# A work order searched anew with other VectorE and buffer costs, and q's weights loaded in three parts

## The chip, the core and the metric

The kernel runs on one core of a Trainium2 chip. TensorE (PE) multiplies, VectorE (DVE) and ScalarE (ACT) empty PSUM and do the elementwise work, GpSimd (POOL) applies masks, and SyncE (SP) issues nearly all DMAs. The metric is the device time of one execution in microseconds; a profile of one execution gives every instruction's start and duration on its own span.

## The reference

Two attention blocks on two inputs of 2048 tokens by 640 features, with 32 heads of 20 features; the outputs stand side by side, 1280 columns wide.

```python
# A: sliding window of 256 tokens
q, k, v = split(A_x @ A_wqkv)
p = softmax(where(0 <= i - j < 256, q @ k.T * 20 ** -0.5, -1e9))
a = (p @ v) @ A_wo
# B: linear attention
q, k, v = split(B_x @ B_wqkv)
phi = lambda t: where(t > 0, t + 1, exp(t)) + 1e-6
kv, z = phi(k).T @ v, phi(k).sum(tokens)
b = ((phi(q) @ kv) / (phi(q) @ z + 1e-6)) @ B_wo
out = concatenate([a, b], -1)
```

## The kernel before

The tokens go in four tiles of 512 (four blocks of 128). All operands are bfloat16, sums are float32 in PSUM.

**A.** Per tile, `proj_pad` (L496) makes q and k with the features in the partitions, five groups of five 512-column products each (L511). The first four groups hold even heads; what belongs to the odd heads goes to DRAM and back in a `relay` (L541, L534, L544, on SP). `proj_v` (L555) makes v (L566). A score *unit* (`unit`, L600) is one head group with part of a tile's key blocks: up to 64 small products in row tiles (L620), two exponentials on ScalarE (L641 for three of four heads, L644 for the fourth), and masks on GpSimd, or on VectorE where the plan says so (L665, L668, L669, L663). There are 96 units; every three give a *value group* (`values`, L689; products in column tiles, L698), copied out (L711) and stored to `orelay` (L730). When a tile's eight value groups are stored, `a_norm` (L740) reads them back (L753, L754), divides, and `finish_rows` (L786, products L796) multiplies by `wo`, copies (L804, L802) and stores to the output (L810).

**B.** `b_keys` (L861, L873) makes 32 key groups of 320 columns, `phi` (L817) follows each. `phi` has two ways: ScalarE takes the exponential straight from PSUM (L826), or VectorE first copies the sum out (L832) and ScalarE works on the copy (L843); then VectorE takes the minimum (L846) and the maximum (L849). `b_sums` (L909) sums over all tokens, `b_kvwo` (L981, L998) folds `wo` in and passes the result through DRAM to `kvwo`, and `b_query` (L1049, L1057, then L796) makes the queries and the result.

**Order of the work.** Nothing of the order is decided on the chip. While the program is built, a planner (`Planner`, L81) keeps a time for every engine and DMA, takes for each engine the ready operation with the lowest key, and emits it; the engines then run these orders strictly, waiting on semaphores. The table `K` (L20) holds the keys, the pace of the units, and the earliest times of DMAs. An operation's planned duration is a formula (`dve_sb`, L256; `phi.min` and `phi.max` at L834 and L835). PSUM offers three fill banks (with the scores' banks when they are free), handed out in turn; a group of products needs the bank whose last user has been read out. Four output buffers (`osb`), four `e` buffers and three `ost` buffers go in rings (`take`, `give`; L235, L236), whose slot the planner counts free at the giving operation's end, for a DMA its landing plus a pad.

**The start.** Ten warm-up products (L1087) run ahead in a fill bank. SP loads x of tile 0 in four blocks (`load_x0`, L455), which TensorE transposes (L470) and VectorE or ScalarE copies (L479). The weights of q and k each come in two column parts, 160 and 480 columns (`load_turned`, L1102), and are copied into their final column order, one copy per group (L1120, L1118). All other tiles of x are transposed by the DMA, five loads per tile (`load_x`, L435; issue at L442). A tile of x takes one of four slots in turn and waits for its former user. B's key weights `wk` are loaded from SP (L1132, L1141).

Of the kernel before, what the change touches and what calls it, by code (L numbers as in the profile page):

```python
# [7 lines left out]
P = 128  # L8
# [5 lines left out]


K = {
    "units": (10.0, 2.45, 0.814, 0.583, 1.081),
    "slack": (0.39, 1.89, 0),
    "defer": 1.27,
    "q0": (-80.4, 1.09),  # L20
    "k0": (-76.5, 0.43),
    "x": (-4.4, -5.1, -9.3, 6.8, 36, 57.2, 100),
    "xb": (129.4, 27.91),
    "w": (1.6, 23.7, 103.0),
    "rows": (86.9, 44, 84, 86.4),
    "pad": 1.41,
    "v0": (-22.4, 0.4),
    "v1": (-69.9, 1.3),
    "q1": (17.3, 1.62),
    "k1": (27.1, 0.69),  # L30
    "b0": (9.7, 0.62),
    "b1": (25.7, 1.09),
    "b2": (55.6, 0.65),
    "b3": (83.3, 0.35),
    "g": (71.6, 7.42),
    "q2": (96.5, 4.88),
    "k2": (45.3, 6.49),
    "v2": (84.0, 1.3),
    "z": (109.3, 0.64),
    "kvwo": (143.1, 1.98),  # L40
    "q3": (116.9, 1.76),
    "k3": (140.6, 0.89),
    "v3": (145.2, 2.04),
    "bq0": (158.1, 2.9, 197.3, 1.46),
    "bq1": (210.9, 4.71, 196.4, 4.76),
    "bq2": (195.1, 0.28, 244.4, 4.78),
    "bq3": (190.6, 2.38, 257.0, 1.47),
    "ao": (8.5, 1.61),
}


# [29 lines left out]
class Planner:  # L81
# [101 lines left out]
    def run(self):  # L183
        while True:
            best = None
            for e, ops in self.avail.items():
                if not ops:
                    continue
                f = self.free.get(e, 0.0)
                t0 = INF  # L190
                for o in ops:
                    s = self._start_time(o, f, e)
                    if s < t0:
                        t0 = s
                if t0 == INF:
                    continue
                t = max(f, t0)
                pick = None
                for o in ops:
                    if self._start_time(o, f, e) <= t + 1e-9:  # L200
                        k = (self._rank(o, t), o.ready)
                        if pick is None or k < pick[0]:
                            pick = (k, o)
                if best is None or t < best[0]:
                    best = (t, e, pick[1])
            if best is None:
                break
            t, e, o = best
            for x in o.engs:
                self.avail[x].remove(o)  # L210
            dur = o.engs[e]
            if e == "PE" and o.mode != self.mode:
                dur += self.SWITCH
                self.mode = o.mode
            if o.group is not None and o.first:
                p = self._bank(t)[1]
                o.group["bank"] = (p, p["next"])
                o.group["pool"] = p["pool"]
                o.group["tag"] = p["tag"]
                p["ends"][p["next"]] = INF  # L220
                p["next"] = (p["next"] + 1) % len(p["ends"])
            for r, h in o.take:
                h["i"] = r["next"]
                r["ends"][r["next"]] = INF
                r["next"] = (r["next"] + 1) % len(r["ends"])
            self.free[e] = t + dur
            o.emit(e)
            if o.mb is not None:
                self.data = max(self.data, t + dur) + o.mb
                self.sent += [self.data + self.LAND] * o.n  # L230
                o.end = self.data + self.LAND + o.pad
            else:
                o.end = t + dur + (self.LAT[e] if o.lat is None else o.lat)
            self.log.append((t, dur, e, o))
            for r, h in o.give:  # L235
                r["ends"][h["i"]] = o.end  # L236
            if o.group is not None and o.last:
                p, i = o.group["bank"]
                p["ends"][i] = o.end
            for s in o.succ:  # L240
                s.ready = max(s.ready, o.end)
                s.left -= 1
                if s.left == 0:
                    self._push(s)
        assert not any(self.avail.values())
# [19 lines left out]
def kernel(  # L265
# [108 lines left out]
            self.users.append(ops)  # L374


    def group(mms, evac, key, deps=(), shape=None, dtype=F32, chunk=2, name="", mode="full"):

        g = {}
        name = name or mms[0][1].__qualname__.split(".<locals>.")[1]  # L380
        prev = None
        n = len(mms)
        i = 0
        first = True
        while i < n:
            part = mms[i : i + chunk]

            def emit(e, part=part, first=first):
                if first:
# [4 lines left out]
            o = pl.op({"PE": sum(m[0] for m in part)}, emit, key if first else -1000, list(deps) if first else [prev], lat=0.0 if i + chunk < n else None, group=g, name=name)  # L394
# [101 lines left out]
    def proj_pad(t, i, key0, dkey):  # L496
# [11 lines left out]
        for c in range(KT):  # L508
            def mk(kt, c=c):
                def m(ps):  # L510
                    nc.tensor.matmul(ps[:], lhsT=wA[i][:, kt, c * P : (c + 1) * P], rhs=xb["t"][:, kt, :], start=(kt == 0), stop=(kt == KT - 1))  # L511
# [305 lines left out]
    def phi(g, n, dst):  # L817
# [5 lines left out]
        def e1(e):  # L823
# [6 lines left out]
            else:  # L830
                st["t"] = epool.tile([P, n], BF16, name="t")
                nc.vector.tensor_copy(out=st["t"][:], in_=g["ps"][:])  # L832
                x = pl.op({"ACT": act_t(n)}, e2, PHK, [o1], name="phi.exp")
            o3 = pl.op({"DVE": 0.14 + 0.00026 * n}, e3, EVK if e == "ACT" else PHK, [x], name="phi.min")  # L834
            o4 = pl.op({"DVE": dve_ps(n) if e == "ACT" else 0.17 + 0.00104 * n}, e4, EVK if e == "ACT" else PHK, [o3], name="phi.max")  # L835
            if e == "ACT":
                o4.group = g
                o4.last = True
# [263 lines left out]
    def load_turned(i, eng, key):  # L1102
# [1 line left out]
        raw = over.tile([P, KT, D], BF16, name="raw", tag=f"K{2 + i}")  # L1104
        v = a[:, :, i * D : (i + 1) * D]
        ld = [load_w(eng, raw[:, :, 0:160], v[:, :, 0:160], key, 0.9, pad=0.5)]
        ld.append(load_w("SP", raw[:, :, 160:], v[:, :, 160:], key + 1, 2.3, pad=0.5))
        wA_op[i] = []
        for c in range(KT):
            def em(e, c=c):  # L1110
# [8 lines left out]
                else:  # L1119
                    nc.vector.tensor_copy(out=d, in_=s)  # L1120

            wA_op[i].append(pl.op({"DVE": dve_sb(D), "ACT": act_t(D)}, em, -5000 if i == c == 0 else -3900 + 2 * c + i, ld[0:1] if c == 0 else ld, name="wturn"))

    load_turned(0, "ACTQ", -99.5)
    load_turned(1, "SP", -99)
# [93 lines left out]
```

## Time and profile before

| | |
|---|---|
| median of 11 runs | 274.89 us (270.7 to 276.0) |
| profiled execution | 275.45 us, its span 273.7 us |
| granted TensorE clock, mean | 0.981 |
| busy: PE, DVE, ACT, POOL | 257.0 (94%), 197.0 (72%), 215.0 (79%), 138.1 (50%) us |
| instructions: PE, DVE, ACT, POOL | 4086, 385, 283, 251 |
| masks on POOL, L668 and L669 | 91 each, mean 673 and 726 ns |
| `phi.min` L846, 320 columns | x32, mean 403 ns |
| `phi.max` L849 from the copy, 320 columns | x22, mean 573 ns |

The span runs from the first to the last instruction; the 1.75 us between it and the execution's time lie around it. A line of the profile names line, engine, operation and tiles; "SPq" is SP's queue issuing a DMA; a bracket at the end holds the engine's idle time ahead of the instruction and what ended it.

### The profile page before, as it was taken

Reading aid. Unit: us, or ns where it says so; the run is one execution under the profiler, and the core shown is the slowest. Engines: PE = TensorE matmul, PEld = TensorE weight load, DVE = VectorE, ACT = ScalarE, POOL = GpSimd, SP = SyncE. Lnnn points to the kernel's source line nnn. Section 1 sums busy time; section 2 is a strip of 40 time slices with the busy share of each in tenths; the row PEclk is TensorE's granted clock in tenths of the full one; section 3 lists DMA queues with packets and bytes.
Section 4 is the critical chain, followed back from the end, with each engine's and each line's share of the span. In section 5 each row is a group of like instructions: output and inputs, shape, how many; then the busy total and the mean of one; then the engine's idle time right before and its main releaser. Section 6 shows DMA issues by size and latency. Waiting matters only on the chain.

```text
span 273.7 us, 9682 instructions
## 1 busy us (share of the span) xinstructions
PE 257.0 (94%) x4086; PEld 153.3 (56%) x4114; DVE 197.0 (72%) x385; ACT 215.0 (79%) x283; POOL 138.1 (50%) x251
## 2 busy tenths in 40 slices
PE   8899999999849999999999999999998899999995
PEld 4336764555514556666555666656555556556673
DVE  2746699978845897634485673667889998789654
ACT  2583099899964998888889888888989899999540
POOL 5056046666553375655555655577783565640000
PEclk9999999999965999999999999999999999999999
DMA  7976969578562494960033367965595234512532
GB/s 206 292 115 118 220 129 215 88 113 235 127 124 57 96 336 131 192 107 22 23 96 100 74 151 210 179 124 109 130 209 181 72 85 103 151 46 69 162 134 96
DMA packets 55996, 37.13 MB, mean 136 GB/s; under 512 B 33681, under 2 KB 55185, under 8 KB 55953
## 3 DMA queue, kind: packets, MB, share of 16 engines
q1 hardware_dynamic: 55297, 36.32, 56.9%
q8 instruction: 32, 0.52, 0.8%
q10 hardware_dynamic: 656, 0.20, 0.3%
q14 instruction: 11, 0.09, 0.1%
HBM read 16.42 MB, written 12.88 MB: 107 GB/s over the span
## 4 chain that ended last, share of the span: by engine, by line
PE 75%; DVE 13%; DMA 6%; issue 2%; SPq 1%; ACT 1%; DVEq 0%; ACTq 0%
PE F L511 16%; PE F L796 13%; PE s L620 9%; PE F L909 8%; PE F L566 8%; PE F L698 8%; PE F L873 5%; PE F L1049 4%; DVE pq L849 3%; DMA raw<-in_A_wqkv_dram 2%; DVE e L846 2%; DVE t L832 2%; DMA xT<-in_A_x_dram 2%; DVE osb L804 2%; DVE ost L711 1%
## 5 line engine op out<-in xcount | busy, mean ns | idle before, releaser
L641 ACT ACTIVATE p<-s 128x1536 bf16<-128x1536 f32 (+2 forms) x96 | 131.8, 1373 | 25.1 <-PE s L620 19.8
L668 POOL TENSOR_SCALAR_AFFINE_SELECT p<-p 128x512 bf16<-128x512 bf16 x91 | 61.3, 673 | 76.4 <-ACT p L641 75.9
L669 POOL TENSOR_SCALAR_AFFINE_SELECT p<-p 128x512 bf16<-128x512 bf16 x91 | 66.1, 726 | 0.0
L511 PE MATMUL F<-xT,wA 128*128 128x512 bf16 x184 | 50.4, 399 | 5.5 <-DMA xT<-in_A_x_dram 2.0
L644 ACT ACTIVATE p<-s 128x512 bf16<-128x512 f32 (+2 forms) x96 | 54.8, 573 | 0.0
L620 PEld LDWEIGHTS <-kpad 20*128 20x128 bf16 x1440 | 21.2, 93 | 31.8 <-issue 30.0
L620 PE MATMUL s<-qpad,kpad 20*128 20x128 bf16 x1440 | 37.6, 219 | 1.3 <-ACT p L641 0.7
L511 PEld LDWEIGHTS <-wA 128*128 128x128 bf16 x200 | 18.1, 100 | 25.4 <-issue 7.9
L711 DVE CAST ost<-F 128x512 bf16<-128x512 f32 x30 | 20.7, 690 | 14.2 <-PE F L698 12.8
L804 DVE CAST osb<-F 128x320 bf16<-128x320 f32 x49 | 23.3, 486 | 8.1 <-PE F L796 6.3
L873 PE MATMUL F<-wkq,xT 128*128 128x320 bf16 x160 | 25.9, 300 | 1.2 <-DVE ost L711 0.8
L1049 PE MATMUL F<-xT,wq 128*128 128x512 bf16 x91 | 24.2, 382 | 2.3 <-DVE t L832 1.0
L698 PE MATMUL F<-p,v 128*32 128x128 bf16 x1440 | 26.0, 220 | 0.1
L796 PE MATMUL F<-woA,oT 128*128 128x320 bf16 x160 | 24.1, 299 | 1.3 <-DVE t L832 1.0
L566 PE MATMUL F<-wA,xT 128*128 128x320 bf16 x160 | 24.8, 299 | 0.0
L665 POOL TENSOR_SCALAR_AFFINE_SELECT p<-p 128x512 bf16<-128x512 bf16 x16 | 10.9, 705 | 26.7 <-ACT p L641 26.7
L796 PE MATMUL F<-kvwo,pq 128*128 128x320 bf16 x160 | 23.5, 299 | 0.2 <-DVE pq L849 0.2
L698 PEld LDWEIGHTS <-v 128*32 128x32 bf16 x1440 | 20.5, 97 | 5.0 <-issue 2.5
L846 DVE TENSOR_SCALAR e<-e 128x320 bf16<-128x320 bf16 (+1 forms) x52 | 20.6, 402 | 2.8 <-ACT e L843 1.6
L832 DVE CAST t<-F 128x320 bf16<-128x320 f32 (+1 forms) x34 | 18.7, 553 | 3.5 <-PE F L1049 1.9
L525 DVE CAST kpad<-F 128x512 bf16<-128x512 f32 x16 | 11.1, 691 | 13.5 <-PE F L511 13.3
L796 PEld LDWEIGHTS <-oT 128*128 128x128 bf16 x160 | 15.1, 98 | 7.9 <-issue 1.2
(77 smaller groups left out, 302.2 us busy)
## 6 DMA issues: line engine op xcount, KB each, us to landing
out_dram<-osb SPq DMA_DIRECT2D x32, 160.0 KB
orelay<-ost SPq DMA_DIRECT2D x32, 128.0 KB
oT<-orelay SPq DMA_DIRECT2D x8, 320.0 KB
qpad<-relay SPq DMA_DIRECT2D x16, 80.0 KB
kpad<-relay SPq DMA_DIRECT2D x16, 80.0 KB
xtok<-in_B_x_dram SPq DMA_DIRECT2D x2, 640.0 KB
xT<-in_B_x_dram SPq DMA_DIRECT2D x2, 640.0 KB
raw<-in_A_wqkv_dram SPq DMA_DIRECT2D x2, 600.0 KB
```

Of the source, the lines that this page charges most:

```text
L511: nc.tensor.matmul(ps[:], lhsT=wA[i][:, kt, c * P : (c + 1) * P], rhs=xb["t"][:, kt, :], start=(kt == 0), stop=(kt == KT - 1))
L566: nc.tensor.matmul(ps[:], lhsT=xb["t"][:, kt, b * P : (b + 1) * P], rhs=wA[2][:, kt, hf * HALF : (hf + 1) * HALF], start=(kt == 0), stop=( ...
L620: nc.tensor.matmul(o, lhsT=kt_[HD * j : HD * j + Dh, hg, ko : ko + P], rhs=qbox["t"][HD * j : HD * j + Dh, hg, b * P : (b + 1) * P], start ...
L641: nc.scalar.activation(out=st["p"][:, 0:3, :, :], in_=st["s3"][:, :, 0 : nb * P].rearrange("p h (k q) -> p h k q", q=P), func=ACT.Exp, sca ...
L644: nc.scalar.activation(out=st["p"][:, 3, :, :], in_=st["s1"][:, 0 : nb * P].rearrange("p (k q) -> p k q", q=P), func=ACT.Exp, scale=scale)
L668: nc.gpsimd.affine_select(out=p[:, :, 0, :], in_=p[:, :, 0, :], pattern=[[0, 4], [-1, P]], compare_op=ALU.is_ge, fill=0.0, base=-1, channe ...
L669: nc.gpsimd.affine_select(out=p[:, :, 1, :], in_=p[:, :, 1, :], pattern=[[0, 4], [1, P]], compare_op=ALU.is_ge, fill=0.0, base=0, channel_ ...
L698: nc.tensor.matmul(ps[HD * j : HD * j + HD, b * P : (b + 1) * P], lhsT=vA[kb]["t"][:, h * HV : h * HV + HD], rhs=pst["p"][:, j, x, :], sta ...
L796: nc.tensor.matmul(ps[:], lhsT=lhs(c), rhs=rhs(c, hf), start=(c == 0), stop=(c == KT - 1))
L804: nc.vector.tensor_copy(out=d, in_=ps[:])
L873: nc.tensor.matmul(ps[:], lhsT=xb["t"][:, kt, b * P : (b + 1) * P], rhs=R["wk"][:, kt, hf * HALF : (hf + 1) * HALF], start=(kt == 0), stop ...
L1049: nc.tensor.matmul(ps[:], lhsT=R["wq"][:, kt, :].rearrange("p (f c) -> p c f", c=KT)[:, c, :], rhs=xb["t"][:, kt, :], start=(kt == 0), sto ...
```

## The change

- **Planner.** `phi.min` and `phi.max` are planned longer (0.14 to 0.25 us and 0.17 to 0.21 us of fixed cost). A ring slot given back by a DMA counts free at the landing, without the pad that other readers wait.
- **Table.** All keys and earliest times are new, `defer` is doubled. Every engine's order changes from the first instructions on. `phi` takes ScalarE's way in 26 of 52 cases instead of 18; of the value copies all 32 stand on VectorE instead of 30.
- **Weights of q.** Three parts: 160 columns on ACT's queue as before, 160 and then 320 columns on SP. Each of the first two groups' copies waits for its own part only.
- **First group of q.** Twenty products of 128 columns, block by block, each block waiting for its own transposed block of x, instead of five of 512 columns.
- **Warm-up.** Five products up front and two placed by the planner between the transposes, in a bank of the scores, instead of ten.
- **`wk`.** Issued from ACT's queue with a very low key, so at its earliest time.

```diff
@@ K (cut)
-    "units": (10.0, 2.45, 0.814, 0.583, 1.081),
+    "units": (12.8, 2.45, 0.773, 0.56, 1.081),
-    "defer": 1.27,
+    "defer": 2.54,
-    "q0": (-80.4, 1.09),
-    "k0": (-76.5, 0.43),
-    "x": (-4.4, -5.1, -9.3, 6.8, 36, 57.2, 100),
-    "xb": (129.4, 27.91),
-    "w": (1.6, 23.7, 103.0),
+    "q0": (-69.9, 0.2),
+    "k0": (-60.2, 0.38),
+    "x": (-8.2, -3.7, -13.5, 1.6, 29.7, 57.2, 100.0),
+    "xb": (135.8, 22.84),
+    "w": (12.5, 36.7, 114.7),
...
@@ Planner.run
-                r["ends"][h["i"]] = o.end
+                r["ends"][h["i"]] = o.end - o.pad
@@ group(..., more=())
-            o = pl.op(..., list(deps) if first else [prev], ...)
+            o = pl.op(..., list(deps) if first else [prev, *more[i // chunk]] if more else [prev], ...)
@@ proj_pad
-            g = group([(mm_t(NQ), mk(kt)) for kt in range(KT)], [(either(NQ), ev)], key0 + c * dkey, deps=list(xb["ready"]) + [wA_op[i][c]] + (need if c < 4 else []))
+            if t == i == c == 0:
+                def mb(b, kt):
+                    def m(ps):
+                        q = slice(b * P, (b + 1) * P)
+                        nc.tensor.matmul(ps[:, q], lhsT=wA[0][:, kt, 0:P], rhs=xb["t"][:, kt, q], start=(kt == 0), stop=(kt == KT - 1))
+                    return m
+
+                g = group([(mm_t(P), mb(b, kt)) for b in range(TB) for kt in range(KT)], [(either(NQ), ev)], key0, deps=xb["ready"][0:1] + [wA_op[0][0]], chunk=KT, more=[[r] for r in xb["ready"]])
+            else:
+                g = group(...)
@@ phi
-            o3 = pl.op({"DVE": 0.14 + 0.00026 * n}, ...)
-            o4 = pl.op({"DVE": dve_ps(n) if e == "ACT" else 0.17 + 0.00104 * n}, ...)
+            o3 = pl.op({"DVE": 0.25 + 0.00026 * n}, ...)
+            o4 = pl.op({"DVE": dve_ps(n) if e == "ACT" else 0.21 + 0.00104 * n}, ...)
@@ start
-    nwarm = 10
+    wt = s3pool.tile([P, 3, NQ], F32, name="s3")
 
     def warmup(e):
-        w = fpool.tile([P, NQ], F32, name="F", tag="bank0")
-        for _ in range(nwarm):
-            nc.tensor.matmul(w[:], lhsT=warm[:, 0:P], rhs=warm[:], start=True, stop=True)
-
-    warmup("PE")
+        nc.tensor.matmul(wt[:, 0, :], lhsT=warm[:, 0:P], rhs=warm[:], start=True, stop=True)
+
+    for _ in range(5):
+        warmup("PE")
+    for at in (3.75, 4.4):
+        pl.op({"PE": 0.43}, warmup, 0, earliest=at)
...
-    pl.free["PE"] = 4.9
+    pl.free["PE"] = 3.4
@@ load_turned
         ld = [load_w(eng, raw[:, :, 0:160], v[:, :, 0:160], key, 0.9, pad=0.5)]
-        ld.append(load_w("SP", raw[:, :, 160:], v[:, :, 160:], key + 1, 2.3, pad=0.5))
+        if i == 0:
+            ld.append(load_w("SP", raw[:, :, 160:320], v[:, :, 160:320], -98.9, 0.9, pad=0.5))
+        r = 160 * len(ld)
+        ld.append(load_w("SP", raw[:, :, r:], v[:, :, r:], key + 1, 1.7 + i * 0.6, pad=0.5))
...
-            wA_op[i].append(pl.op(..., ld[0:1] if c == 0 else ld, name="wturn"))
+            wA_op[i].append(pl.op(..., ld[c : c + 1] if c < len(ld) - 1 else ld, name="wturn"))
@@ wk
-    wk_op = dma("SP", em_wk, 3.0, -94, at=K["w"][0])
+    wk_op = dma("ACT", em_wk, 3.0, -9000, at=K["w"][0])
```

More of the change, by code (lines that the diff above doesn't have):

```diff
@@ L16 @@
 K = {
-    "units": (10.0, 2.45, 0.814, 0.583, 1.081),
+    "units": (12.8, 2.45, 0.773, 0.56, 1.081),
     "slack": (0.39, 1.89, 0),
-    "defer": 1.27,
-    "q0": (-80.4, 1.09),
-    "k0": (-76.5, 0.43),
-    "x": (-4.4, -5.1, -9.3, 6.8, 36, 57.2, 100),
-    "xb": (129.4, 27.91),
-    "w": (1.6, 23.7, 103.0),
[L25 to L39, printed above, removed]
-    "kvwo": (143.1, 1.98),
[L41 to L48, printed above, removed]
+    "defer": 2.54,
[4 more added lines that the diff above has]
+    "w": (12.5, 36.7, 114.7),
+    "rows": (97.4, 62.8, 73.4, 101.8),
+    "pad": 1.5,
+    "v0": (-29.6, 0.51),
+    "v1": (-75.5, 0.43),
+    "q1": (23.6, 1.01),
+    "k1": (25.8, 0.69),
+    "b0": (6.6, 0.77),
+    "b1": (25.7, 1.29),
+    "b2": (56.0, 0.36),
+    "b3": (85.0, 0.35),
+    "g": (70.3, 7.63),
+    "q2": (86.4, 3.69),
+    "k2": (49.1, 9.21),
+    "v2": (82.2, 1.44),
+    "z": (102.5, 1.81),
+    "kvwo": (143.1, 1.98),
+    "q3": (118.7, 1.04),
+    "k3": (140.6, 1.47),
+    "v3": (140.8, 2.04),
+    "bq0": (158.1, 2.68, 197.3, 0.97),
+    "bq1": (210.0, 4.04, 187.1, 0.32),
+    "bq2": (192.2, 0.36, 240.5, 4.77),
+    "bq3": (190.6, 0.23, 271.1, 2.36),
+    "ao": (10.8, 0.85),
 }
@@ L374, in add, with group @@
             self.users.append(ops)
-    def group(mms, evac, key, deps=(), shape=None, dtype=F32, chunk=2, name="", mode="full"):
+    def group(mms, evac, key, deps=(), shape=None, dtype=F32, chunk=2, name="", mode="full", more=()):
         g = {}
@@ L392, in emit @@
                     m(g["ps"])
-            o = pl.op({"PE": sum(m[0] for m in part)}, emit, key if first else -1000, list(deps) if first else [prev], lat=0.0 if i + chunk < n else None, group=g, name=name)
+            o = pl.op({"PE": sum(m[0] for m in part)}, emit, key if first else -1000, list(deps) if first else [prev, *more[i // chunk]] if more else [prev], lat=0.0 if i + chunk < n else None, group=g, name=name)
             o.first = first
@@ L525, in ev @@
                     nc.vector.tensor_copy(out=d, in_=ps[:])
-            g = group([(mm_t(NQ), mk(kt)) for kt in range(KT)], [(either(NQ), ev)], key0 + c * dkey, deps=list(xb["ready"]) + [wA_op[i][c]] + (need if c < 4 else []))
+            if t == i == c == 0:
[6 more added lines that the diff above has]
+            else:
+                g = group([(mm_t(NQ), mk(kt)) for kt in range(KT)], [(either(NQ), ev)], key0 + c * dkey, deps=list(xb["ready"]) + [wA_op[i][c]] + (need if c < 4 else []))
             xb["users"].append(g["mm"])
@@ L833, in e1 @@
                 x = pl.op({"ACT": act_t(n)}, e2, PHK, [o1], name="phi.exp")
-            o3 = pl.op({"DVE": 0.14 + 0.00026 * n}, e3, EVK if e == "ACT" else PHK, [x], name="phi.min")
-            o4 = pl.op({"DVE": dve_ps(n) if e == "ACT" else 0.17 + 0.00104 * n}, e4, EVK if e == "ACT" else PHK, [o3], name="phi.max")
+            o3 = pl.op({"DVE": 0.25 + 0.00026 * n}, e3, EVK if e == "ACT" else PHK, [x], name="phi.min")
+            o4 = pl.op({"DVE": dve_ps(n) if e == "ACT" else 0.21 + 0.00104 * n}, e4, EVK if e == "ACT" else PHK, [o3], name="phi.max")
             if e == "ACT":
@@ L1120, in em @@
                     nc.vector.tensor_copy(out=d, in_=s)
-            wA_op[i].append(pl.op({"DVE": dve_sb(D), "ACT": act_t(D)}, em, -5000 if i == c == 0 else -3900 + 2 * c + i, ld[0:1] if c == 0 else ld, name="wturn"))
+            wA_op[i].append(pl.op({"DVE": dve_sb(D), "ACT": act_t(D)}, em, -5000 if i == c == 0 else -3900 + 2 * c + i, ld[c : c + 1] if c < len(ld) - 1 else ld, name="wturn"))
     load_turned(0, "ACTQ", -99.5)
```

## The prediction

> **What bounds the kernel now.** I read the page first (span, busy rows, clock row), then TensorE's waits, then the busy time by stage, then the timeline around the one place that these point to. The page:
>
> ```profile
> span 273.7 us, 9682 instructions
> ...
> PE   8899999999849999999999999999998899999995
> ...
> PEclk9999999999965999999999999999999999999999
> ```
>
> A slice is 6.8 us. TensorE is busy nearly everywhere; the twelfth slice (75 to 82 us) is more than half empty, and in it and the next the granted clock drops. Busy time by stage (window, length, then busy time and count of PE, PEld, DVE, ACT, POOL, the clock, DMA):
>
> ```profile
> 74.00:77.50 3.50, 1.68 (x45) 1.13 (x38) 3.35 (x6) 3.50 (x7) 3.35 (x6) 0.99 0.63 163
> 77.50:82.00 4.50, 2.04 (x5) 0.65 (x5) 1.07 (x3) 1.89 (x3) 1.65 (x3) 0.50 0.55 100
> 82.00:87.60 5.60, 5.24 (x42) 1.88 (x41) 2.26 (x5) 2.27 (x3) 2.18 (x4) 0.50 0.29 70
> ...
> 207.00:254.00 47.00, 45.01 (x797) 28.10 (x806) 42.92 (x84) 45.07 (x62) 21.92 (x30) 1.00 0.34 101
> ```
>
> From 77.5 to 87.6 TensorE runs at half clock. From 207 to 254 ScalarE (45.1 of 47) is as full as TensorE. What stopped TensorE near 78, from its waits and the timeline:
>
> ```profile
> PE F L511 <- DMA xT<-in_A_x_dram: 2.0, 1, 2.0
> ...
> PE F L511 <- DVE t L832: 1.1, 1, 1.1
> ```
>
> ```profile
> 66.47 2.07 SPq L541 DMA_DIRECT2D relay<-kpad  x4
> ...
> 69.94 2.19 SPq L442 DMA_TRANSPOSE xT<-in_A_x_dram  x1
> ...
> 72.30 1.52 SPq L544 DMA_DIRECT2D kpad<-relay  x4
> ...
> 73.87 1.13 SPq L442 DMA_TRANSPOSE xT<-in_A_x_dram  x1
> ...
> 75.67 3.74 SPq L442 DMA_TRANSPOSE xT<-in_A_x_dram  x3
> ...
> 81.39 1.44 PE L511 MATMUL F<-xT,wA 128*128 128x512 bf16 x3 [2.02 <-DMA xT<-in_A_x_dram]
> ```
>
> The k product of A's token tile 2 stands in TensorE's order at 76.8, but its five transposed loads leave SP's queue between 69.9 and 79.4, behind the relay of tile 1's k; the last lands at about 81.3. Everything behind it in TensorE's order waits too.
>
> How much is that? TensorE's steady spacing is in the chain of waits: 100 products of 320 columns in 13.66 us, 136 ns each; 512 columns take 216 ns, a 16-block score unit 0.23, a 48-block value group 0.79. Counted on from 10.25 us with 0.098 us for each change between whole, row-tile and column-tile products (the fit), the order before gives the recorded starts of all seven value groups from 33.9 to 66.7 us within 0.1 us, so nothing else is lost up to there. Between the value groups at 73.4 and 87.8 (14.4 us) stand 6.2 us of such work: **8.1 us lost**. The same sum shows 1.0 lost in the interval ahead, 3.5 from 191 to 253, and little else. So TensorE is the bound, with one large hole.
>
> [...] of the 7.3 us busy in those two stages half is lost, some 3.6 of the 8.1. [...] `phi.min` (L846, 320 columns) takes 0.23 at times and 1.05 for two beside GpSimd's masks, mean 0.403, while the planner counted 0.22 (now 0.33). [...]
>
> **Part 1, the head.** From the timeline of the start:
>
> ```profile
> 7.83 3.45 PE L511 MATMUL F<-xT,wA 128*128 128x512 bf16 x14 [0.94 <-DVE xT L479]
> ...
> 9.47 1.35 ACT L1118 COPY wA<-raw 128x640 bf16<-128x640 bf16 x2 [2.38 <-DMA raw<-in_A_wqkv_dram]
> ```
>
> Before: ten warm-up products fill TensorE from 1.25 to 5.5; transposes of x; the last VectorE copy ends 7.8; q's first group of products runs 7.83 to 8.9, k's to 10.0; q's second group waits for the 600 KB second part of its weights (landed 9.45) and ScalarE's turn (0.73), and starts at 10.25.
> After: five warm-ups end at 1.25+5×0.427=3.4; four transposed blocks and two single warm-ups alternate (a warm-up of 512 columns takes 0.427 at this point, so five of 128 take 0.53; 4×0.53+2×0.43=3.0) to about 6.4, x's blocks having landed at 3.2, 3.7, 5.2 and 5.7 before. The 20 products of 128 columns (20×56=1.12 us, against 5×216=1.08; fifteen more weight loads at 100 ns run beside) start as the first blocks are copied and end soon after the last copy, 7.1. k's first group follows until 8.3. q's second group needs only the new 200 KB part; at the pace of the 600 KB (which followed the part landed at 6.34, so 3.1 us) it lands by 7.5 and is turned by VectorE by about 8.3. q's third needs the last part, near 9.4, turned by 9.8. So at 9.85 TensorE has one group (1.08) more behind it than before at 10.25: **−1.5 us**. The order's total of TensorE work falls by the same three warm-ups (232.5 to 231.3 without changes, of which there are 227 and 228).
>
> **Part 2, wk on ACT's queue.** It stands between the two exponentials of the third score unit and waits for the fifth transposed load of A's tile 1 (landed 17.8 before). That unit's scores come at 16.5 by the sum and its first exponential ends near 18.1, so 0 to 0.6 plus 0.5 of issue falls on ScalarE. Behind it: the unit's second exponential and the next two units; TensorE would feel it at the fifth score unit, near 20.6. TensorE has v products in front of that, hence 0; 1 us if they run out. Two margins are thin: v of tile 1 now comes 1.8 us earlier in TensorE's order and meets those loads at 18.5, while the third weight part puts one more issue (0.46) ahead of them on SP; and keys' block 0 of B has its fifth load behind the relays (near 29.5, landing 31) where TensorE needs it at 31.4. I take 0.2 for both, bounds 0 and 2; below zero is excluded, as nothing there waited before.
>
> **Part 3, the hole.** In SP's new order tile 1's q relay no longer stands behind seven transposed loads (it left at 57.0, ten us after its data). Following that order with 0.35 to 0.4 per relay, 0.53 per store and 1.25 per transposed load: q relay near 53, k relay 57 to 59, its reads from 61.5 (after 2 us of landing), `xtok` 63.2, the five loads of tile 2 from 63.8, held once by a value store (66.2), the fifth issued at 69.3. With the 3.2 us from issue to landing of the fifth load before: 72.5. TensorE needs that block at 72.2. Ahead of it stand fewer `phi` chains: seven of the 32 key chains change from VectorE's copy (0.49) to ScalarE reading PSUM, and only one chain of the last key tile (B's tile 3) precedes instead of two. ScalarE's steps (1.33+0.48 per unit, 0.34 to 0.38 per `phi`) in the four intervals there sum to 6.3, 6.9, 6.5, 7.2 against TensorE's 6.0, 7.0, 5.9, 9.4, so it no longer lags (before: 7.3 and 6.2 against 6.2 and 4.9). Of the 9.1 lost (8.1 and the 1.0 ahead) I keep 3.0: 1.0 for the load, which meets its need within 0.3 us, [...] and 1.0 for what the smaller waits then put late; no half clock[...]. Bounds 0.5 and 9.1. **−6.1**.
>
> **Part 4, the last third.** From units 72 to 96 ScalarE has the same steps as before (58.2 us both times); the stretch took 62. TensorE's order holds 2.4 us less in it and 1.6 more after the last value group (18.3 against 16.7). ScalarE sets the pace, so the work moved behind it is not saved: 60.4+18.3 against 62+16.7, **0**; bounds −2.2 (ScalarE at its floor) and +1.6 (still 62). The end, 3.5 us from last product to last store, stays. Counting buffers free at landing changes no wait; four output buffers and stores every 1.4 us leave room: 0.
>
> Sum on the profiled execution: 275.45 − 1.5 + 0.2 − 6.1 + 0 = **268.0**. The profiled execution lies 0.6 above the median 274.89 of the eleven runs (270.7 to 276.0), which I leave as it is.
>
> **Rivals.**
> - *Forecast*, 265.5 to 270.5: hole mostly gone, head gained. 0.53.
> - *Deeper*: the hole shrinks to 0.5 and the last third goes half way to ScalarE's floor: 275.45−1.5+0.2−8.6−1.1 = 264.4. For: `phi.min` is now planned nearer its measured 0.403. Against: ScalarE and VectorE are coupled there and idled 4 us. 0.13.
> - *One smaller stall is left* (a thin margin of part 2 or the hole at 4 to 5 us without half clock): 270.5 to 272. 0.04.
> - *The hole stays*: tile 2 lands over 3 us later than worked out, [...] the clock halves again: 275.45−1.5 = 273.9, or with the margins of part 2 some 277. For: the margin is about zero and SP's queue is in order. Against: every step ahead of it is earlier. 0.20.
> - *Slower, by a late last B tile.* Its products move up 9.5 us in TensorE's order. On SP its third load stands behind an output store that needs the copy of a product which ends 9.3 us before TensorE needs the tile. Copy 0.5, store 0.35, three loads 2.6 to the last issue, landing 3.2: 6.7, so 2.7 to spare. It decides when the loads come over 2.7 late; slower than 277.6 needs 9.6 more, a wait of 4.6 and 5 of half clock, so 7.3 late. For: transposed loads have taken 2 to 3.4 to issue. Against: queue rows are light there (DMA 0.34). 0.10.
> - *It doesn't do what it says* in the head, if parts land no earlier: 269.5, inside the forecast.
>
> **Numbers.** About 1% can be told from no change here, so faster is under 272.1, slower over 277.6. Faster 0.53+0.13+0.04 = 0.70; same 0.20; slower 0.10. The 8 in 10 range takes in the deeper case and most of the staying hole: 264.3 to 274.5; the likeliest alone 265.5 to 270.5.
>
> **What would show it.** Head: q's second product near 8.4, third near 9.85. Hole: no slice with a clock under 9 between 70 and 90, the wait for `xT<-in_A_x_dram` under 1 us, value groups near 71 and 79. Last third: ScalarE over 95% busy to the last value group, then 18.3 us of products. Wrong if the clock row dips anywhere after the start, if TensorE waits over 2 us for one transposed load, or if ScalarE's exponentials wait behind `wk`.

## The result and the profile after

| | before | after |
|---|---|---|
| median | 274.54 us (47 runs, 270.4 to 276.3) | 268.99 us (12 runs, 267.1 to 271.4) |
| profiled execution, its span | 275.45, 273.7 us | 267.96, 266.2 us |
| granted clock in it | 0.981 | 1.000 |

The ratio of the undisturbed runs is **0.989 (95% interval 0.985 to 0.993)**; it leaves out runs over 1.5% above the fastest of their kernel, which takes out most of those near 275 us of the kernel before: of its 47 runs 21 are kept, 16 at 270.4 to 271.6 and five at 273.5 to 274.2 us. In absolute time the forecast of 268.0 was 1.0 us off. The gain that it named, 2.5%, did not come: it is 1.1% by this ratio, and 2.0% between the two medians. Why these differ is what the runs had to find out.

The page after, with the lines that answer to those of before:

```profile
span 266.2 us, 9712 instructions
...
PE   8999998999979999999999999999999889999995
...
PEclk9999999999999999999999999999999999999999
```

In this execution the half-empty slice and the dip of the clock are gone. The waits of TensorE say how much of the hole is left (in total, times, longest):

```profile
PE s L629 <- ACT p L650: 1.2, 3, 0.8
PE F L707 <- DVE pk L858: 1.2, 2, 0.9
PE F L511 <- DMA xT<-in_A_x_dram: 1.2, 2, 1.0
```

Line numbers are nine higher in the middle of the file. TensorE still waits for the transposed loads of A's tile 2, 1.2 us in two pieces; the 0.9 us for `pk` (the keys after `phi`), at 41 us, is new. The hole and the last third by stage (columns as before: window, length, PE, PEld, DVE, ACT, POOL, clock, DMA):

```profile
74.50:77.90 3.40, 2.19 (x22) 0.75 (x23) 1.16 (x4) 2.48 (x5) 3.40 (x6) 1.00 0.50 81
77.90:82.00 4.10, 4.08 (x77) 2.00 (x76) 3.79 (x10) 3.77 (x5) 0.32 (x2) 1.00 0.54 189
198.00:245.00 47.00, 44.18 (x772) 26.98 (x780) 44.12 (x83) 45.29 (x60) 24.81 (x36) 1.00 0.36 107
```

Where TensorE had 1.68 of 3.50 us and then ten microseconds of half clock, it now has one stretch with 2.19 of 3.40. SP's queue shows why (start, length):

```profile
65.43 1.55 SPq L553 DMA_DIRECT2D kpad<-relay  x4
67.02 0.40 SPq L908 DMA_DIRECT2D xtok<-in_B_x_dram  x1
67.53 3.39 SPq L442 DMA_TRANSPOSE xT<-in_A_x_dram  x2
71.02 0.52 SPq L739 DMA_DIRECT2D orelay<-ost  x1
71.60 3.73 SPq L442 DMA_TRANSPOSE xT<-in_A_x_dram  x3
```

The relay of tile 1's k is read back before the loads and not between them, and the fifth load has left the queue at 75.3 instead of 79.4. (`xtok` is a load of rows of B's x, 640 KB.)

### The profile page after: what moved, and what is told of

It is laid out like the page before. It is cut to its first block, busy times and chain, and to the rows that moved or that the text cites. A ratio compares the mean times of both kernels' runs of the same rounds, so it can differ in the third digit from the quotient of the medians.

```text
span 266.2 us, 9712 instructions
## 1 busy us (share of the span) xinstructions
PE 253.2 (95%) x4098; PEld 153.9 (58%) x4126; DVE 194.7 (73%) x381; ACT 212.4 (80%) x278; POOL 137.0 (51%) x253
## 4 chain that ended last, share of the span: by engine, by line
PE 79%; DVE 9%; ACT 5%; SPq 2%; issue 2%; DMA 2%; ACTq 0%; DVEq 0%
PE F L805 16%; PE F L511 15%; PE s L629 10%; PE F L918 9%; PE F L575 8%; PE F L707 8%; PE F L1058 4%; PE F L882 4%; ACT p L650 3%; DVE e L855 3%; DVE pq L858 2%; SPq L442 2%; PE F L1066 1%; PE s L1094 1%; DMA xT<-in_A_x_dram 1%
## 5 line engine op out<-in xcount | busy, mean ns | idle before, releaser
L511 PE MATMUL F<-xT,wA 128*128 128x512 bf16 x177 | 46.3, 381 | 2.6 <-DMA xT<-in_A_x_dram 1.2
L720 DVE CAST ost<-F 128x512 bf16<-128x512 f32 x32 | 22.1, 689 | 15.3 <-PE F L707 13.5
L813 DVE CAST osb<-F 128x320 bf16<-128x320 f32 x52 | 25.0, 487 | 8.1 <-PE F L805 7.5
L511 PEld LDWEIGHTS <-wA 128*128 128x128 bf16 x195 | 17.3, 98 | 19.1 <-DVE wA L1133 0.8
L575 PE MATMUL F<-wA,xT 128*128 128x320 bf16 x160 | 25.6, 300 | 0.0
L882 PE MATMUL F<-wkq,xT 128*128 128x320 bf16 x160 | 25.3, 300 | 0.2
L589 DVE CAST v<-F 128x320 bf16<-128x320 f32 x32 | 15.8, 492 | 5.8 <-PE F L575 5.5
L575 PEld LDWEIGHTS <-xT 128*128 128x128 bf16 x160 | 14.9, 98 | 7.3
L835 ACT ACTIVATE e<-F 128x320 bf16<-128x320 f32 (+1 forms) x26 | 13.1, 502 | 7.4 <-PE F L882 7.3
```

The lines of the kernel that those rows point to most:

```text
L575: nc.tensor.matmul(ps[:], lhsT=xb["t"][:, kt, b * P : (b + 1) * P], rhs=wA[2][:, kt, hf * HALF : (hf + 1) * HALF], start=(kt == 0), stop=( ...
L882: nc.tensor.matmul(ps[:], lhsT=xb["t"][:, kt, b * P : (b + 1) * P], rhs=R["wk"][:, kt, hf * HALF : (hf + 1) * HALF], start=(kt == 0), stop ...
```

## The experiments

**The kernel before again.** No edit; each execution with its clock.

> The kernel before, unchanged, timed again with the granted clock of each execution beside its time. Theory: its executions fall in two groups, about 271 us and about 275 us, and the difference is the half clock alone: clock 0.98 (10.24 us at half, some 3.6 to 4 us lost) in the upper group, 0.998 or more in the lower. Rival: the two groups come from something else (transposed loads landing later, say), and the clock is the same within 0.004 in both.

Here, and in all executions of the kernel before that ran beside the experiments, the granted clock takes steps. The traces show why: away from the kernel's end, half clock comes in whole windows of 3.413 us (10.24, 6.83 and 3.41 us in three traces), and in a trace the steps lie whole windows apart: in the profiled execution before, full clock for 71.68 us (21 windows), half for 10.24 (3), full for 187.73 (55), the first full window beginning at 5.73 us. So the mean clock counts the windows, (1 - clock) x span x 2 / 3.413, rounded:

| half-clock windows | 0 | 1 | 2 | 3 | mean |
|---|---|---|---|---|---|
| before: executions | 6 | 27 | 36 | 15 | 1.71 windows |
| mean time, us | 269.7 | 271.3 | 274.2 | 275.1 | 273.1 |
| after (three sets of runs) | 13 | 7 | 2 | 0 | 0.50 windows |
| mean time, us | 267.8 | 270.3 | 271.2 | | 268.9 |

The kernel before alone spans 269.1 to 276.3 us with one and the same program. The profiled execution of the prediction had three windows, as 15 of these 84 had. At equal clock the change is worth 1.9 us (no window) or 1.0 us (one); the two executions of the changed kernel with two windows are 3.0 us below those of the kernel before. With the changed kernel's mix of windows the kernel before would average 270.6 us: so of the 4.2 us between the means some 2.5 go with the fewer windows and 1.7 are there at an equal number. This is a count and not a clean split, since what makes a window also takes time itself.

What brings a window about can be read by asking for TensorE's busy time in the windows of this grid. The kernel before, first in the profiled execution, then in this one:

```profile
74.00:77.41 3.41, 1.68 (x45) 1.13 (x38) 3.26 (x6) 3.41 (x7) 3.26 (x6) 1.00 0.62 161
77.41:80.82 3.41, 1.44 (x3) 0.40 (x3) 1.16 (x4) 1.98 (x3) 1.74 (x3) 0.50 0.60 99
80.82:84.24 3.42, 2.49 (x21) 0.98 (x22) 1.33 (x3) 0.34 (x1) 0.00 (x0) 0.50 0.34 77
84.24:87.65 3.41, 3.41 (x24) 1.15 (x22) 0.98 (x2) 1.93 (x3) 2.23 (x4) 0.50 0.29 78
```

```profile
73.97:77.38 3.41, 1.41 (x33) 0.89 (x22) 3.41 (x6) 3.41 (x7) 3.26 (x6) 1.00 0.68 165
77.38:80.80 3.42, 1.44 (x3) 0.41 (x3) 0.88 (x3) 1.70 (x3) 1.47 (x3) 0.50 0.54 91
80.80:84.21 3.41, 3.15 (x22) 1.04 (x22) 1.33 (x3) 0.64 (x1) 0.00 (x0) 0.50 0.43 109
```

TensorE is not idle in the window ahead of the drop: it is busy for 1.68 and 1.41 of 3.41 us. Over all traces of this case, away from the kernels' ends, each of the 16 windows with a busy share of 0.54 or less was followed by half clock, and none at full clock with 0.61 or more. (At the end of two traces, windows with 0.52 and 0.54 kept full clock, so the border is not sharp.) So several small waits in one window are enough (in the first trace 0.46, 0.70 and the first 0.57 of a wait of 1.09 us); it takes no single long one. The second trace came back after one window less, TensorE being busy for 3.15 us of its second half-clock window against 2.49; over all traces a share of 0.86 and more ended half clock, 0.76 and less did not, and of two windows between, 0.82 did and 0.83 did not.

**Filling the hole of before.**

```diff
+ if (t, i, c, kt) == (2, 1, 0, 0):
+     for _ in range(12):
+         nc.tensor.matmul(ps[:], lhsT=wA[1][:, 0, 0:P], rhs=wA[1][:, 0, 0:NQ], start=True, stop=True)
```

> The kernel before with twelve products of 512 columns that nothing reads, 2.6 us of work, ahead of the first k product of A's tile 2, where TensorE otherwise stands idle for the transposed loads. Theory (the half clock is a consequence of the idle time there): the clock stays full and nearly every execution is at the lower group of the kernel before, 270.5 to 271.5 us, ratio to the undisturbed ones 0.998 to 1.002; no execution near 275. Rival 1 (the half clock comes from elsewhere): two groups stay, 271 and 275. Rival 2 (the hole's waits are full of other work): 2.6 us are added, 273.5 us.

272.82 us (271.7 to 273.6), ratio 1.008 (1.002 to 1.014). Two executions without a window (272.0), two with one (273.4), none near 275. The filler stood too late: the window that decided had ended at 76.9 in this trace, and the filler began at 77.4. It cut what followed, from two or three windows to one or none, but where no window falls it costs 2.3 us against 269.7. Theory and second rival are each half right.

**One part alone, planned anew.** The diff's head (warm-up, weights in parts, `more`, products by blocks) put into the old kernel and taken out of the new one, and the same with the planner's numbers:

```diff
-                r["ends"][h["i"]] = o.end
+                r["ends"][h["i"]] = o.end - o.pad
...
-            o3 = pl.op({"DVE": 0.14 + 0.00026 * n}, e3, ...
+            o3 = pl.op({"DVE": 0.25 + 0.00026 * n}, e3, ...
```

> The kernel before with only the new head: single warm-up products, q's weights in three parts, the first products by blocks; the table, the planner's durations and the place of wk as before. Theory (head and hole add up): 1.0 to 1.5 us less than before in executions of equal clock, 269.5 to 270.2 us where the clock is full, the hole still there. Rival (the head's gain is given back at the next late load): 270.8 to 271.3 us, no change.

> The changed kernel with only the head undone: ten warm-up products, q's weights in two parts, the first products whole. Theory: 1.0 to 1.5 us more than the changed kernel, 268.5 to 270 us in executions with full clock, some 0.994 of the undisturbed kernel before. Rival 1 (the new head brought nothing): 267.1 to 268 us. Rival 2 (all the gain is the head's): 271 us.

> The kernel before with only the planner's numbers changed: VectorE's SBUF steps longer and output buffers free at landing; table and head as before. The order is planned anew from them. Theory (the table was searched for one set of durations, so a new set with the old table gives an order that nobody chose, as with the head alone, which cost 5 us): 272 to 282 us at full clock or with one window. Rival (truer durations alone give the better order): 266 to 269 us.

> The changed kernel with only the planner's numbers put back: VectorE's SBUF steps short, output buffers free half a landing later; the new table and the new head stay. Theory (as with the old head in the new table, which cost 7 us, an order that nobody chose): 271 to 280 us. Rival (the durations hardly matter, the table does it): 267 to 269 us.

Medians 276.32, 275.34, 278.44 and 277.71 us: ratios to the kernel before 1.022, 1.016, 1.026 and 1.025, all four intervals above 1.009. The first two expectations were wrong by 5 us and more; the last two held in time, though not in the clock that the third named (no half-clock window or one): six of their eight executions have three. A part changes what the planner plans, the order of every engine moves, and waits appear in places that neither kernel has. The waits of the last one:

```profile
PE F L805 <- DVE osb L813: 3.5, 2, 2.9
PE s L629 <- ACT p L650: 2.2, 3, 1.0
PE F L805 <- DVE pq L1083: 2.0, 1, 2.0
```

So the table fits one set of durations and one head, and such a run does not tell a part's own worth. From here on the order of every engine was kept, and only what the planner's operations emit was changed.

**The head, order kept.** What is planned stays, what it emits changes. In the old order: five warm-ups ahead and one behind each of the first two transposed blocks, q's second load as two, and the blocks at the fifth product's place. In the new order: all of that back.

```diff
+ if t == i == c == 0:
+     for b in range(TB if kt == KT - 1 else 0):
+         q = slice(b * P, (b + 1) * P)
+         for k in range(KT):
+             nc.tensor.matmul(ps[:, q], lhsT=wA[0][:, k, 0:P], rhs=xb["t"][:, k, q], ...)
+     return
...
-        ld.append(load_w("SP", raw[:, :, 160:], v[:, :, 160:], key + 1, 2.3, pad=0.5))
+            cut = (160, 320, D) if i == 0 else (160, D)
+            for x, y in zip(cut, cut[1:]):
+                nc.sync.dma_start(out=raw[:, :, x:y], in_=v[:, :, x:y])
```

> The kernel before with its order of instructions kept on every engine and only the head's instructions changed: five warm-up products and two between the transposed blocks, q's weights in three parts, the first products by blocks. (With the same edit made in the planner's input the whole order moved, and the run told nothing of the head.) Theory: the head is worth 1.1 us, as the first value group (33.9 against 32.8 us) shows: 268.1 us at full clock, 270 us with one half-clock window. Rival 1 (given back at the late loads): 269.2 us at full clock. Rival 2 (the old order cannot use it): slower.

> The changed kernel with its order of instructions kept and only the head's instructions as before: ten warm-up products, q's weights in two parts, the first products whole. Theory: 1.1 to 1.6 us slower than the changed kernel, 268.5 to 269 us at full clock, so the 7 us that the re-planned kernel with the old head lost came from its other order, mostly in the last third. Rival (the head itself is worth 7 us to this order): 274 to 275 us.

In the new order the head is worth what the theory said: without it 269.05 us where no window falls (15 executions) against 267.78, **1.3 us**. The start of q's first groups with the head and without it:

```profile
6.53 1.60 PE L531 MATMUL F<-xT,wA 128*128 128x128 bf16 x20
7.97 3.76 PE L511 MATMUL F<-xT,wA 128*128 128x512 bf16 x15
```

```profile
8.40 1.24 PE L531 MATMUL F<-xT,wA 128*128 128x512 bf16 x5 [0.70 <-DVE xT L479]
9.47 2.90 PE L511 MATMUL F<-xT,wA 128*128 128x512 bf16 x12
```

But without it only 2 of 17 executions have windows, against 9 of 22: TensorE comes later, and in the trace it waits 0.3 us for the loads of tile 2 instead of 1.2. The median, 269.25, is just 0.3 above 268.99. In the old order no gain of the head is seen at one window: 271.37 us (four executions) against 271.28. The profiled execution has two windows, as that of the kernel before again, and takes 273.56 us against 273.59, with the first value group at 33.6 us in both. Eleven executions with two windows do average 272.5 us against 274.2, which these traces do not explain. The timeline of this run:

```profile
7.35 1.24 PE L521 MATMUL F<-xT,wA 128*128 128x512 bf16 x5
...
9.12 1.35 ACT L1132 COPY wA<-raw 128x640 bf16<-128x640 bf16 x2 [2.02 <-DMA raw<-in_A_wqkv_dram]
...
9.89 1.04 PE L521 MATMUL F<-xT,wA 128*128 128x512 bf16 x4 [1.30 <-ACT wA L1132]
```

The old order turns q's second group on ScalarE only when the last part of the weights is there; TensorE waits 1.30 us and goes on at 9.89, against 10.25 before, and by the first value group nothing is left of that. The head's gain needs the order as well as the loads.

**k of tile 2 on resident data, order kept.**

```diff
- rhs=xb["t"][:, kt, :]
+ rhs=(R["B0"] if t == 2 and i == 1 else xb)["t"][:, kt, :]
```

> The kernel before with its order kept, but the k products of A's tile 2 read B's tile 1, which has long been in SBUF, in place of A's tile 2 (so k of that tile is computed from other data); the transposed loads of A's tile 2 are still issued. Theory (the late loads make the hole and most of the half clock): no wait of TensorE for xT of A_x; at most one half-clock window, left over from the 2.3 us of smaller waits ahead; nearly all executions at 267.5 to 270.5 us, no execution at 273 to 276. Rival (the smaller waits for VectorE and ScalarE make the half clock by themselves): two groups stay, the upper at 272 us or more.

> The kernel before with its order kept, and the k products of A's tile 2 reading B's tile 0, whose buffer is not the one that the late loads write (in the run with B's tile 1 it was, and the loads then stood on SP until those products had ended); k of that tile is so computed from other data. Theory (late loads make the hole): no wait of TensorE for xT in the k products; one half-clock window at most, left from the 2.3 us of smaller waits between 74 and 78; 268 to 270.5 us in every execution. Rival (the smaller waits are enough for two or three windows): an upper group at 272 us or more.

> The changed kernel with its order kept, and the k products of A's tile 2 reading B's tile 0, long in SBUF (k of that tile is so computed from other data). Theory (the loads' waits are 1.2 to 1.9 us, but what follows them is then held by the next item that is late): no half-clock window in any execution, and 266.7 to 268 us, so at most 1 us off the 267.9 us of undisturbed clock. Rival (the waits are lost in full): 265.7 to 266.6 us.

The first try, on B's tile 1, failed by its own doing: that is the tile whose slot the late loads overwrite. They stood on SP until the k products had ended, at 87 us, and made a larger hole (286.57 us). With B's tile 0 the kernel before takes 270.45 us (269.5 to 271.4), two executions with one window, two with none, ratio 0.988 (0.982 to 0.993), none at 273 or more, where 51 of the 84 executions with the loads have two windows or three: the loads do make the second and third window. But at equal clock it takes 269.5 and 271.4 us, as the kernel before does with them (269.7 and 271.3). And one window remains, from waits of 0.46, 0.70 and 1.1 us for VectorE and ScalarE alone:

```profile
75.00:78.42 3.42, 1.62 (x24) 0.94 (x24) 3.39 (x7) 3.42 (x6) 3.27 (x6) 1.00 0.60 135
78.42:81.83 3.41, 3.41 (x24) 1.14 (x23) 1.53 (x4) 1.49 (x4) 0.75 (x2) 0.50 0.70 109
```

The changed kernel on resident data takes 267.07 us (266.6 to 267.6) and has no window: 1.8 us below its mean with the loads, 0.7 below its executions without a window.

**The rest of the hole.** Order kept but for SP's queue: `xtok` and one store of values behind the loads of tile 2 (first), two of the loads ahead of the relay of k (second), `xtok` alone behind the loads (third and fourth; the fifth is the changed kernel beside it). In the planner, with k the number of the operation (466 is `xtok`, 519 the fifth load):

```diff
-            o.emit(e)
+            k = len(self.log)
+            if k == 466:
+                kept = o
+            else:
+                o.emit(e)
+            if k == 519:
+                kept.emit("SP")
```

> The changed kernel with its order kept but for two entries of SP's queue: the load of xtok (0.40 us) and one store of values (0.52 us), which stand ahead of and between the transposed loads of A's tile 2, come right behind them. Theory (what is left of the hole is the loads' lateness, and it decides whether a half-clock window falls): the loads are issued some 0.9 us earlier, TensorE's waits for them fall from 1.2 to 1.9 us to 0.3 to 1.0, 267 to 267.8 us at full clock, and executions with a half-clock window become rare (1 in 4 or fewer, against 6 in 16). Rival (the store or xtok is needed early): as slow as the changed kernel or slower.

> The changed kernel with its order kept but for two of the five transposed loads of A's tile 2, which are issued ahead of the relay of tile 1's k, where SP waits for that k. Theory: the fifth load is issued over 2 us earlier, no wait of TensorE over 0.3 us for xT of A_x, no half-clock window, 266.2 to 267.2 us in every execution. Rival (the relay of k comes later by what the two loads take, and TensorE then waits for kpad): 268 to 270 us.

> The changed kernel with its order kept but for the load of xtok, which comes behind the transposed loads of A's tile 2 (the store of values stays between them, since behind them it made the read of nA, and ScalarE with it, 1.4 us late). Theory: loads 0.4 us earlier, 267.2 to 267.9 us at full clock, fewer executions with a half-clock window than 6 in 16. Rival (0.4 us changes nothing): the same times and windows as the changed kernel.

> The version with xtok behind the loads once more, with more executions. Theory (0.4 us decide the window): no half-clock window in at least 5 of 6 executions, median 267.3 to 268. Rival (chance): as many windows as the changed kernel beside it.

> The changed kernel on the same chip. Theory: 267.2 to 268.3 us at full clock, a third of the executions with one half-clock window at 269.5 to 271.5 us. Rival (the windows belong to the chip, not to the kernel): none here, and no difference from the version with xtok behind the loads.

The first has no window in four executions and yet takes 268.87 us, above the changed kernel's 267.8 where that has none. ScalarE's timeline shows where the time went:

```profile
85.42 0.47 ACT L859 ACTIVATE e<-t 128x320 bf16<-128x320 bf16 x1
87.31 0.63 ACT L776 ACTIVATE den<-nA 128x512 f32<-128x512 bf16 x1 [1.42 <-DMA nA<-orelay]
87.85 1.43 ACT L657 ACTIVATE p<-s 128x1536 bf16<-128x1536 f32 x1
```

TensorE gets past the hole 1.3 us earlier (value group at 80.0 instead of 81.3), and ScalarE waits 1.42 us for `nA`, the sums that `a_norm` reads back; the exponential behind it, and TensorE's unit (1.25 us), wait too. The next value group but one starts at 96.8, 0.2 later than in the changed kernel. `nA` is late because its read is: SP's queue in the changed kernel, then in this run:

```profile
76.05 0.45 SPq L739 DMA_DIRECT2D orelay<-ost  x1
80.50 0.57 SPq L762 DMA_DIRECT2D oT<-orelay  x1
81.12 0.59 SPq L763 DMA_DIRECT2D nA<-orelay  x1
```

```profile
75.79 0.62 SPq L746 DMA_DIRECT2D orelay<-ost  x1
82.78 0.57 SPq L769 DMA_DIRECT2D oT<-orelay  x1
83.40 0.59 SPq L770 DMA_DIRECT2D nA<-orelay  x1
```

The reads wait until the store has landed, and SP waits 6.3 us for that instead of 3.9. In this run `xtok`, the other moved store and a second load of 640 KB are issued within 1.7 us ahead of it; in the changed kernel `xtok` is issued 9 us ahead. So this run's order of SP's queue made `nA` late; that it did so by putting `xtok` there is likely, but no run tested it alone. The second was wrong altogether, 274.28 us, with two windows or three in every execution:

```profile
SPq L447 <- PE F L887: 6.9, 2, 6.2
```

The tile's slot is still in use by B's products: SP stood at the first load until 63.9 us, with the relay of k behind it, and TensorE later waited 5.6 us for the fifth. `xtok` alone has no window in ten executions against 9 in 22, so 0.4 us of a queue entry seem enough to avoid it. But its gain is not kept: beside each other both take 268.88 us. In that run too the read of `nA` is late (82.3 us, against 81.2 in the changed kernel beside it) and ScalarE waits 1.52 us for it, though the store of values kept its place; in the third run's trace the read is issued at 81.4, and ScalarE does not wait.

**wk, order kept,** back on SP's queue.

```diff
-        q_of(e).dma_start(out=R["wk"][:], in_=wBv[:, :, D : 2 * D])
+        nc.sync.dma_start(out=R["wk"][:], in_=wBv[:, :, D : 2 * D])
```

> The changed kernel with its order kept, and only the load of B's k weights back on SP's queue, at the place where it stands in time. Theory (the load's queue decides nothing, 0 to 0.5 us either way): 267.3 to 268.5 us at full clock. Rival 1 (its place on ScalarE's queue costs the predicted 0.2 to 2 us): 266 to 267.3 us. Rival 2 (the 0.58 us on SP delay the loads and relays behind it): slower by over 0.5 us.

269.42 us; 269.2 where no window falls (three executions), against 267.8 of the changed kernel on this chip (three too): the second rival. The one execution with a window took 270.8 us, against 270.3, so the 1.4 us stand on few runs. On SP everything behind moves: the read of q's relay takes 3.68 instead of 1.70 us, with a wait that the profile puts down to `wk` itself:

```profile
SPq L553 <- DMA wkq<-in_B_wqkv_dram: 1.5, 1, 1.5
```

The relay of tile 1's q leaves at 57.45 instead of 54.89, and the fifth load of tile 2 has left at 76.2 instead of 75.3. TensorE feels none of it up to the value group at 72.1, which starts when it does in the changed kernel; the next one comes at 83.6, and at 83.4 in the changed kernel's own trace with a window.

**The changed kernel again.**

> The changed kernel, unchanged, again, to have its executions beside those of the kernel before with the clock of each. Theory: at equal clock it is 1 to 2 us faster (269.2 against 267.4 us at full clock, 271.1 against 269.5 to 271 us with one half-clock window of 3.41 us); what the medians show beyond that is that the kernel before has two or three half-clock windows in many of its executions and the changed one has none or one. Rival: at equal clock it is 4 us or more faster.

268.18 us (267.0 to 271.1), ratio 0.989 (0.981 to 0.998). At equal clock it is as the table above has it, 1 to 2 us with no window or one; the rival's 4 us is excluded there. Its trace has one window, after a stretch of TensorE with 1.62 of 3.42 us busy:

```profile
75.21:78.63 3.42, 1.62 (x21) 0.64 (x21) 0.83 (x3) 1.75 (x5) 2.59 (x5) 1.00 0.49 90
```

The same waits as in the trace shown first, 1.9 instead of 1.2 us, on another phase of the grid.

## Why the prediction was right and wrong

- **The failed step is the base of the sum.** "The profiled execution lies 0.6 above the median 274.89 of the eleven runs (270.7 to 276.0), which I leave as it is." Four of those eleven runs were at 270.7 to 271.4 us: the kernel had two levels, and the profile showed the upper one, with three half-clock windows. Between executions with three windows and with one lie 3.8 us, about the 3.6 that Part 3 booked as half clock and took as gained in full. That is right for a pair of executions (275.45 and 267.96 differ by 7.5, forecast 7.4), and that this pair was met is luck: three windows against none, as 15 of 84 and 13 of 22 executions have them. It is wrong for the undisturbed runs, of which 16 in 21 lie where the table has no window or one: at these levels the change is worth 1.9 and 1.0 us, and the kernel before on resident data (269.5, 271.4) shows that the late loads cost nothing more there.
- **Part 1, head, -1.5.** Mechanism right, 1.3 measured. At 10.25 us TensorE has one group more behind it; the starts of q's second and third group, 9.2 and 10.3 us, came later than the 8.4 and 9.85 forecast, in part since the products by blocks took 1.6 us and not 1.12: seven of the twenty ran ahead of the first full clock, at 7.2, 107 ns apart. The two groups started as VectorE's copies of their weights ended. Not foreseen: in the old order no gain is seen at one window, and in the new one it makes tile 2's loads later for TensorE.
- **Part 2, wk, +0.2.** Wrong sign: with its load on SP the kernel is some 1.4 us slower where no window falls (three executions each). The exponentials felt nothing: none waits behind `wk`'s issue at 17.4 us.
- **Part 3, the hole, -6.1.** By the same sum 2.4 us are lost in the interval up to 81.3 and about 0.2 in the one ahead; 3.0 were forecast for both, 1.0 of them for VectorE by an estimate that no run showed. The value groups came at 72.1 and 81.3 (71 and 79). So the total was right for the profiled pair, but not by the path described. The issue of the fifth load began at 74.1 and it landed at 76.8, and not at 69.3 and 72.5: over 4 us late, as the rival "The hole stays" had it. But TensorE's fifth product, without waits, would have stood at 75.3 and not at 72.2. Two errors of 3 to 4 us cancelled, and the wait was 1.2 us. Wrong was also "no half clock" beside 3.0 us of waits: how long a wait would have to be for it was an assumption that no trace had shown. Waits of 1.0 and 0.9 us made a window in the changed kernel, and the kernel before gets one without its late loads.
- **Part 4, last third, 0.** 59.3 + 18.0 us against 60.4 + 18.3 forecast and 62 + 16.7 before; 1.4 us better. ScalarE at 45.3 of 47 us is still as full as TensorE.
- The rivals "The hole stays" and "Slower, by a late last B tile" did not come; B's last tile made no wait.

Open: why the loads come earlier in some executions than in others; no trace of the kernel before without a window was taken. And what else the new order is worth: at equal clock the head (1.3) and `wk`'s queue (1.4, on few runs) together exceed the 1.9 us, so the parts don't add up, and the rest, the planner's two new costs among it, was not separated.

## What to carry to other kernels

If the runs of one program fall in levels, find out which level the profile is of before a sum is made against it, and count its half-clock windows. Add up TensorE's idle time per window (3.413 us here, and half clock after 0.54 or less of it busy), not per wait. To test a part of a planned kernel, keep the order and change what is emitted; and when an entry of a queue is moved, look at what it then stands in front of (here a store, and the read of `nA` that waits for it), since that can take the gain back.

## What was not expected of the hardware

- Away from the kernels' ends, half clock followed each window of 3.413 us in which TensorE was busy for 0.54 or less of it (16 windows, from 0 to 0.54; the next above, 0.61, kept full clock; two at the ends, 0.52 and 0.54, kept it too). The grid's phase to the program differs between executions (the first full window began at 4.0 to 7.2 us), and one program had none to three half-clock windows.
- One window costs 1.6 us in the kernel before (269.7 to 271.3) and 2.5 in the changed one (267.8 to 270.3), where 1.7 would be half of its length. In the changed kernel's traces TensorE waits 1.9 and 1.8 us for the loads where there is a window, and 1.2 where there is none.
- One DMA issue of 0.58 us more on SP at 22 us moved later entries of that queue by up to 2.6 us, with a relay's read that took 3.68 instead of 1.70 us.
